# Seven products for every pair of row blocks in a mixture-of-experts stage, with each chunk's first sums on VectorE

## The chip, the cores and the metric

The kernel runs on one core of one Trainium2 chip. The core has a matrix engine (TensorE), a vector engine (VectorE, DVE in the profile), a scalar engine (ScalarE, ACT), a general engine (GpSimd, POOL) and a queue engine for transfers (SyncE, SP). Each engine works through its own queue in order, and semaphores tie the queues together. The metric is the time of one execution on the device, in microseconds; times of several executions are given by their median.

## The reference

The program is a sorted block attention followed by a dense mixture of eight experts. The attention gives 3072 rows `x` of 512 numbers. A softmax over the gate `x @ w_gate` is balanced by eight rounds of row and column normalisation, which gives weights `P`. All experts see all rows:

```python
out = np.zeros((N, D), dtype=np.float32)       # N, D, E, F = 3072, 512, 8, 1024
for e in range(E):
    h = np.maximum(x @ w1[e], 0.0)
    ye = h @ w2[e]
    out += P[:, e:e + 1] * ye
```

The first product is `x @ w1[e]` (512 deep, 1024 wide), the second `h @ w2[e]` (1024 deep, 512 wide). Everything the change touches lies in this loop, for experts 1 to 7; expert 0 is worked off beside the attention.

## The kernel before

The rows are cut into three chunks of 1024 (`p` = 0, 1, 2). For each expert and chunk the hidden tile `hT` is made in four units (`hidden`, i = 0 to 3) of seven products each, after the scheme of Strassen and Winograd: the matrices are seen as 2 x 2 blocks, and seven block products of sums take the place of eight. One product is two matmuls of 512 columns. The seven go into three PSUM banks of the pool `bk` (5 banks); ScalarE copies partial sums out (L502, L510, L515) and makes the last block (L524), VectorE makes the three other blocks by adding such a copy to a bank (L506 after product 2, L518 after product 5, L521 after product 6). The sums of weights that this needs are made by GpSimd (`sum_w`, L330), those of `x` by VectorE (`sum_x`, L434).

The second product of a chunk has four units too, i = 0 to 3. A unit makes two row blocks of 128 rows, `i` and `4 + i` (a pair), and comes in two forms:

- `output` (L536) is the plain form: two times eight matmuls of 512 columns (L542), each group in one bank of the pool `op` (3 banks). When a group is done, `gather` (L529) multiplies it by the expert's weight column and adds it to the output rows `osbl` on VectorE, 512 wide.
- `output7` (L561) uses seven products of four matmuls, 256 columns each (L573), on two banks: `u`, on which products 1, 3, 5 and 7 accumulate with a 256-wide gather after each, and `x`, whose left half takes product 2 and whose right half products 4 and 6; the right half is gathered after product 4, the whole bank (512 wide) after product 6. Product 3 needs the sum `s2` of four hidden blocks, 4 needs `s1`, 5 needs `s3`, 6 needs `s4`. `sum_h` (L553) makes the four on GpSimd, each 512 elements a partition (4 blocks f of 128), and `sum_w2` (L423) makes the sums of `w2`.

The sums s1 to s4 of unit i need all of `hT`, thus the last `hidden` unit of the chunk. The main loop (L639) takes the hidden units of chunk n and the second product's units of chunk n - 1 side by side: `take` alternates one step of each. At i = 0 the second product is plain, since the sums of that unit could only start when `hT` is complete; for i = 1 to 3 GpSimd makes the sums one unit ahead (`sum_h(i + 1, ...)`). In the first chunk (n = 1) and the last chunk all four units are plain. So of 84 units 57 use seven products and 27 are plain.

GpSimd's queue also holds the loads of `w1` and `w2` (L84, L89) for the expert after the next, at the start and the end of the chunk in which an expert begins, and the weight sums, which `sums` deals out at one a unit, three in the last unit. Matmuls, VectorE's work and the sums of `hT` may be moved by the scheduler within what their data allow; the loads and the weight sums are pinned to the order of the program.

Of the kernel before, what the change touches and what calls it, by code (L numbers as in the profile page):

```python
# [14 lines left out]
BF16 = mybir.dt.bfloat16  # L15
# [10 lines left out]
def kernel(  # L26
# [11 lines left out]
    nc = tc.nc  # L38
# [43 lines left out]
    def load_w1(e):  # L82
        w1t[e] = wp.tile([128, 4, F], BF16, name="w1e")
        pin(nc.gpsimd.dma_start(out=w1t[e],  # L84
                                in_=moe_w1[e].rearrange("(kk k) f -> k kk f", k=128)))

    def load_w2(e):
        w2t[e] = (wq if e else wcp).tile([128, 8, Dm], BF16, name="w2e")
        pin(nc.gpsimd.dma_start(out=w2t[e],  # L89
                                in_=moe_w2[e].rearrange("(fb k) f -> k fb f", k=128)))  # L90
# [231 lines left out]
    def sum_w(e):  # L322
        wct[e] = (wcq if e % 2 == 0 else wcp).tile([128, 3, 2, F // 2], BF16, name="wc")
        for kk in range(2):
            a11, a21 = (w1t[e][:, kk, f:f + 512] for f in (0, 512))
            a12, a22 = (w1t[e][:, 2 + kk, f:f + 512] for f in (0, 512))
            s1, s2, s4 = (wct[e][:, j, kk, :] for j in range(3))
            for a, b, o, c in ((a21, a22, ALU.add, s1), (s1, a11, ALU.subtract, s2),
                               (a11, a21, ALU.subtract, a21), (a12, s2, ALU.subtract, s4)):
                pin(nc.gpsimd.tensor_tensor(out=c, in0=a, in1=b, op=o))  # L330
                yield
# [83 lines left out]
    def sum_w2(e):  # L415
        w2s[e] = (wcp.tile([128, 4, 4, Dm // 2], BF16, name="w2e") if e % 2 else
                  w2q.tile([128, 4, 4, Dm // 2], BF16, name="w2s"))
        for k in (0, 2):
            b11, b12 = (w2t[e][:, k:k + 2, d:d + 256] for d in (0, 256))
            b21, b22 = (w2t[e][:, 4 + k:6 + k, d:d + 256] for d in (0, 256))  # L420
            t1, t2, t3, t4 = (w2s[e][:, j, k:k + 2, :] for j in range(4))
            for a, b, c in ((b12, b11, t1), (b22, t1, t2), (b22, b12, t3), (b21, t2, t4)):
                pin(nc.gpsimd.tensor_tensor(out=c, in0=a, in1=b, op=ALU.subtract))  # L423
                yield
# [111 lines left out]
    def output(e, p, i, hT):  # L536
        for j in range(2):
            tt = 4 * j + i
            t = 8 * p + tt
            oacc = op.tile([128, Dm], F32, name="oacc")  # L540
            for fb in range(8):
                nc.tensor.matmul(oacc, hT[:, fb, tt * 128:(tt + 1) * 128],  # L542
                                 w2t[e][:, fb, :], start=(fb == 0), stop=(fb == 7))
                if fb % 2 and fb < 7:
                    yield
            gather(e, t, 0, oacc)
            store(e, t)
            yield
# [1 line left out]

    hs = {}

    def sum_h(i, hT):  # L553
        s = hs[i] = hsp.tile([128, 4, 4, 128], BF16, name="hs")
        a11, a21, a12, a22 = (hT[:, f:f + 4, t + 128 * i:t + 128 * i + 128]
                              for f in (0, 4) for t in (0, 512))
        for a, b, o, c in ((a21, a22, ALU.add, 0), (s[:, 0], a11, ALU.subtract, 1),
                           (a11, a21, ALU.subtract, 2), (a12, s[:, 1], ALU.subtract, 3)):
            nc.gpsimd.tensor_tensor(out=s[:, c], in0=a, in1=b, op=o)  # L559

    def output7(e, p, i, hT):  # L561
        a, b = 8 * p + i, 8 * p + 4 + i
# [37 lines left out]
    def scale0(ts):  # L600
        for t in ts:
            nc.scalar.activation(out=osbl[:, t, :], in_=osbl[:, t, :], func=AF.Copy,
                                 scale=glog[:, t, 0:1])

    def take(works):
        while works:
            works = [w for w in works if next(w, 0) is None]
# [18 lines left out]
            next(xs, 0)  # L626
    take([chain, xs])
    xs = sum_x(2)
    last = (1, 0, hT)
    queue = [sum_w2(1)]  # L630

    def sums(n):
        while n and queue:
            if next(queue[0], 0) is None:
                n -= 1
            else:
                queue.pop(0)

    for n in range(1, 3 * (E - 1)):  # L639
        e, p = 1 + n // 3, n % 3  # L640
        if n == 1 or p == 0 and e + 1 < E:
            load_w1(e + 1)
            queue.append(sum_w(e + 1))
        hT = htp.tile([128, 8, 1024], BF16, name="hT")
        for i in range(4):
            if last[0] == 1:
                scale0([8 * last[1] + i, 8 * last[1] + 4 + i])
            if n > 1 and i < 3:
                sum_h(i + 1, last[2])
            next(xs, 0)  # L650
            sums(3 if n == 1 or i == 3 else 1)
            take([hidden(e, p, i, hT),
                  (output7 if n > 1 and i else output)(*last[0:2], i, last[2])])
        if n == 1 or p == 0 and e + 1 < E:
            load_w2(e + 1)
            queue.append(sum_w2(e + 1))
        last = (e, p, hT)
    for i in range(4):
        take([output(*last[0:2], i, last[2])])


# [28 lines left out]
```

## Time and profile before

| | us |
|---|---|
| median of 3 runs (lowest, highest) | 690.83 (690.35, 691.81) |
| the profiled execution | 690.48 |
| its span in the profile | 688.7 |
| TensorE matmul busy | 666.7 (97%) |
| VectorE busy | 474.5 (69%) |
| ScalarE busy | 298.0 (43%) |
| GpSimd busy | 432.4 (63%) |
| last plain units, L542 x64 | 13.98, from 670.08 |

A group's line in the profile gives source line, engine, operation, output and input tiles, shapes and count, then busy time with the mean of one in ns, then the idle time before the group and what ended it. A timeline's line gives start, duration, engine, line and operation. Matmuls are pipelined, so their single durations overlap; distances between starts say more. Idle time of an engine that is not the bottleneck costs nothing.

### The profile page before, as it was taken

Reading aid. Unit: us, or ns where it says so; the run is one execution under the profiler, and the core shown is the slowest. Engines: PE = TensorE matmul, PEld = TensorE weight load, DVE = VectorE, ACT = ScalarE, POOL = GpSimd, SP = SyncE. Lnnn points to the kernel's source line nnn. Section 1 sums busy time; section 2 is a strip of 40 time slices with the busy share of each in tenths; the row PEclk is TensorE's granted clock in tenths of the full one; section 3 lists DMA queues with packets and bytes.
Section 4 is the critical chain, followed back from the end, with each engine's and each line's share of the span. In section 5 each row is a group of like instructions: output and inputs, shape, how many; then the busy total and the mean of one; then the engine's idle time right before and its main releaser. Section 6 shows DMA issues by size and latency. Waiting matters only on the chain.

```text
span 688.7 us, 12265 instructions
## 1 busy us (share of the span) xinstructions
PE 666.7 (97%) x4784; PEld 404.4 (59%) x4784; DVE 474.5 (69%) x968; ACT 298.0 (43%) x550; POOL 432.4 (63%) x411
## 2 busy tenths in 40 slices
PE   2999999999999999999999999999999999999997
PEld 1757666644446556556656655655665665565563
DVE  6627555578757778667767776767776777676773
ACT  3747646345953333343333433333333433334330
POOL 4532324202737987978977987789795998637520
PEclk9899999999999999999999999999999999999999
DMA  9897833403210340030302140034003120001213
GB/s 146 164 218 120 140 77 63 62 1 62 30 32 1 62 61 1 1 63 9 54 0 35 28 62 1 1 62 61 1 1 62 25 38 0 1 1 63 91 65 151
DMA packets 31755, 36.51 MB, mean 53 GB/s; under 512 B 2000, under 2 KB 24016, under 8 KB 31696
## 3 DMA queue, kind: packets, MB, share of 16 engines
q0 software_dynamic: 26400, 27.82, 25.5%
q1 hardware_dynamic: 5296, 7.90, 3.4%
q8 instruction: 37, 0.61, 0.4%
q14 instruction: 22, 0.18, 0.1%
HBM read 52.45 MB, written 6.29 MB: 85 GB/s over the span
## 4 chain that ended last, share of the span: by engine, by line
PE 91%; DVE 5%; ACT 1%; DMA 1%; issue 1%; SPq 0%; DVEq 0%
PE bk L482 36%; PE oacc L573 25%; PE oacc L542 13%; PE bank L297 5%; PE bank L304 5%; PE bank L232 2%; PE bank L152 1%; PE bank L243 1%; PE bank L215 1%; PE bank L196 1%; DMA vsb<-vs 1%; DVE cs L464 0%; PE bk L297 0%; PE bk L466 0%; PE bank L183 0%
## 5 line engine op out<-in xcount | busy, mean ns | idle before, releaser
L529 DVE SCALAR_TENSOR_TENSOR osbl<-oacc,glog,osbl 128x256 f32<-128x256 f32 (+1 forms) x396 | 214.8, 554 | 122.4 <-PE oacc L542 61.3
L559 POOL TENSOR_TENSOR hs<-hT 128x512 bf16<-128x512 bf16 x114 | 130.0, 1154 | 63.0 <-DVE hT L521 62.8
L482 PE MATMUL bk<-xtT,w1e 128*128 128x512 bf16 x504 | 149.9, 379 | 0.2 <-ACT u L510 0.2
L573 PEld LDWEIGHTS <-hs 128*128 128x128 bf16 x912 | 89.2, 98 | 59.0
L542 PE MATMUL oacc<-w2e,hT 128*128 128x512 bf16 x432 | 119.8, 379 | 0.0
L524 ACT ACTIVATE hT<-bk 128x512 bf16<-128x512 f32 x84 | 50.1, 597 | 153.0 <-PE bk L482 152.9
L482 PE MATMUL bk<-xc,wc 128*128 128x512 bf16 x336 | 99.9, 379 | 0.0
L573 PEld LDWEIGHTS <-hT 128*128 128x128 bf16 x684 | 66.9, 98 | 44.2
L510 ACT COPY u<-bk 128x512 f32<-128x512 f32 x84 | 49.2, 586 | 92.9 <-PE bk L482 92.8
L573 PE MATMUL oacc<-w2e,hs 128*128 128x256 bf16 x588 | 88.2, 273 | 0.0
L573 PE MATMUL oacc<-w2e,hT 128*128 128x256 bf16 x576 | 86.4, 273 | 0.0
L482 PEld LDWEIGHTS <-w1e 128*128 128x128 bf16 x672 | 65.8, 98 | 30.5 <-issue 1.4
L542 PEld LDWEIGHTS <-hT 128*128 128x128 bf16 x432 | 42.3, 98 | 50.8
L506 DVE CUSTOM_DVE_ANT_0 hT<-bk,p 128x512 bf16<-128x512 f32 x84 | 58.0, 691 | 18.4 <-PE bk L482 14.8
L559 POOL TENSOR_TENSOR hs<-hT,hs 128x512 bf16<-128x512 bf16 x57 | 65.8, 1154 | 1.5
L559 POOL TENSOR_TENSOR hs<-hs,hT 128x512 bf16<-128x512 bf16 x57 | 65.7, 1152 | 0.0
L502 ACT COPY p<-bk 128x512 f32<-128x512 f32 x84 | 49.2, 586 | 31.3 <-PE bk L482 31.3
L482 PEld LDWEIGHTS <-wc 128*128 128x128 bf16 x504 | 49.3, 98 | 22.2
L518 DVE CUSTOM_DVE_ANT_0 hT<-bk,p 128x512 bf16<-128x512 f32 x84 | 57.8, 688 | 4.5 <-PE bk L482 1.4
L515 ACT COPY p<-bk 128x512 f32<-128x512 f32 x84 | 49.3, 586 | 25.4 <-PE bk L482 25.4
L521 DVE CUSTOM_DVE_ANT_0 hT<-bk,u 128x512 bf16<-128x512 f32 x84 | 57.3, 682 | 0.1
L482 PE MATMUL bk<-xc,w1e 128*128 128x512 bf16 x168 | 50.0, 379 | 0.0
(106 smaller groups left out, 777.6 us busy)
## 6 DMA issues: line engine op xcount, KB each, us to landing
w1e<-in_moe_w_dram POOLq DMA_DIRECT2D x8, 1024.0 KB, 8.2
w2e<-in_moe_w_dram POOLq DMA_DIRECT2D x8, 1024.0 KB, 8.9
out_dram<-osbl SPq DMA_DIRECT2D x24, 256.0 KB, 2.0
vt<-in_v_dram POOLq DMA_DIRECT2D x3, 768.0 KB, 10.6
vsb<-vs SPq DMA_DIRECT2D x16, 97.5 KB, 4.6
vsb<-vs POOLq DMA_DIRECT2D x16, 97.5 KB, 4.1
qt<-in_q_dram POOLq DMA_DIRECT2D x4, 384.0 KB, 12.8
kt<-in_k_dram POOLq DMA_DIRECT2D x4, 384.0 KB, 13.4
```

Of the source, the lines that this page charges most:

```text
L482: nc.tensor.matmul(ps, wa[:, kk, :], xa[:, kk, :], start=(first and kk == 0), stop=(kk == 1), skip_group_check=True)
L502: nc.scalar.copy(p1, u)
L506: nc.vector._custom_dve(TENSOR_ADD_SAT, out=c11, in0=w, in1=p1, s0=TOP, s1=0.0)
L510: nc.scalar.copy(u2, u)
L515: nc.scalar.copy(p5, v)
L518: nc.vector._custom_dve(TENSOR_ADD_SAT, out=c22, in0=u, in1=p5, s0=TOP, s1=0.0)
L521: nc.vector._custom_dve(TENSOR_ADD_SAT, out=c12, in0=v, in1=u2, s0=TOP, s1=0.0)
L524: nc.scalar.activation(out=c21, in_=u, func=AF.Relu)
L529: nc.vector.scalar_tensor_tensor(out=o, in0=ps, scalar=glog[:, t, e:e + 1], in1=o, op0=ALU.mult, op1=ALU.add)
L542: nc.tensor.matmul(oacc, hT[:, fb, tt * 128:(tt + 1) * 128], w2t[e][:, fb, :], start=(fb == 0), stop=(fb == 7))
L559: nc.gpsimd.tensor_tensor(out=s[:, c], in0=a, in1=b, op=o)
L573: nc.tensor.matmul(ps, h[:, fb, :], w[:, fb, :], start=(first and fb == 0), stop=(fb == 3), skip_group_check=True)
```

## The change

All 84 units of the second product use `output7`. The four plain units at the start and the end of the experts and the plain unit 0 of each chunk in between are gone.

The sums of unit 0 are made by VectorE, in two parts: those of blocks f = 0 to 2 (384 elements a partition, four operations), which need the first three hidden units only, are issued beside unit 3 of the chunk before, and those of f = 3 (128 elements, four operations) beside unit 0 itself. `sum_h` gets the range of f and the engine as arguments and becomes a generator that yields after each operation. Units 1 to 3 keep their sums on GpSimd.

The hidden units of all chunks become one stream, `ahead`, which is started two products before the second product's first unit; each step of `output7` is then followed by one product of that stream, and by one sum of `mine` where there is one. The last chunk has no hidden work beside it. The eight sums of `w2` of expert 1 are made before the loop. Loads keep their place by chunk.

```diff
-    def sum_h(i, hT):
-        s = hs[i] = hsp.tile([128, 4, 4, 128], BF16, name="hs")
-        a11, a21, a12, a22 = (hT[:, f:f + 4, t + 128 * i:t + 128 * i + 128]
+    def sum_h(i, hT, f0=0, f1=4, eng=nc.gpsimd):
+
+        if f0 == 0:
+            hs[i] = hsp.tile([128, 4, 4, 128], BF16, name="hs")
+        s = hs[i][:, :, f0:f1]
+        a11, a21, a12, a22 = (hT[:, f + f0:f + f1, t + 128 * i:t + 128 * i + 128]
                               for f in (0, 4) for t in (0, 512))
         for a, b, o, c in ((a21, a22, ALU.add, 0), (s[:, 0], a11, ALU.subtract, 1),
                            (a11, a21, ALU.subtract, 2), (a12, s[:, 1], ALU.subtract, 3)):
-            nc.gpsimd.tensor_tensor(out=s[:, c], in0=a, in1=b, op=o)
+            eng.tensor_tensor(out=s[:, c], in0=a, in1=b, op=o)
+            yield
...
-    last = (1, 0, hT)
     queue = [sum_w2(1)]
+
+    def run(*works):
+        for w in works:
+            for _ in w:
+                pass
...
-    for n in range(1, 3 * (E - 1)):
-        e, p = 1 + n // 3, n % 3
-        if n == 1 or p == 0 and e + 1 < E:
-            load_w1(e + 1)
-            queue.append(sum_w(e + 1))
-        hT = htp.tile([128, 8, 1024], BF16, name="hT")
+    sums(8)
+    run(sum_h(0, hT, 0, 3, nc.vector))
+    hTs = {0: hT}
+
+    def hiddens():
+        for n in range(1, 3 * (E - 1)):
+            hTs[n] = htp.tile([128, 8, 1024], BF16, name="hT")
+            yield from units(1 + n // 3, n % 3, hTs[n])
+
+    ahead = hiddens()
+    for _ in range(2):
+        next(ahead)
+    for n in range(1, 3 * (E - 1) + 1):
+        e, p, hT = 1 + (n - 1) // 3, (n - 1) % 3, hTs[n - 1]
+        d = 2 + n // 3
+        fetch = n == 1 or n % 3 == 0 and d < E
+        if fetch:
+            load_w1(d)
+            queue.append(sum_w(d))
+        if n == 3 * (E - 1):
+            run(sum_h(0, hT, 3, 4, nc.vector), sum_h(1, hT), sum_h(2, hT))
         for i in range(4):
-            if last[0] == 1:
-                scale0([8 * last[1] + i, 8 * last[1] + 4 + i])
-            if n > 1 and i < 3:
-                sum_h(i + 1, last[2])
+            if e == 1:
+                scale0([8 * p + i, 8 * p + 4 + i])
             next(xs, 0)
-            sums(3 if n == 1 or i == 3 else 1)
-            take([hidden(e, p, i, hT),
-                  (output7 if n > 1 and i else output)(*last[0:2], i, last[2])])
-        if n == 1 or p == 0 and e + 1 < E:
-            load_w2(e + 1)
-            queue.append(sum_w2(e + 1))
-        last = (e, p, hT)
-    for i in range(4):
-        take([output(*last[0:2], i, last[2])])
+            mine = iter(())
+            if n < 3 * (E - 1):
+                if i < 3:
+                    run(sum_h(i + 1, hT))
+                sums(3 if i == 3 else 1)
+                if i == 0:
+                    mine = sum_h(0, hT, 3, 4, nc.vector)
+                elif i == 3:
+                    mine = sum_h(0, hTs[n], 0, 3, nc.vector)
+            elif i == 1:
+                run(sum_h(3, hT))
+            for _ in output7(e, p, i, hT):
+                next(ahead, 0)
+                next(mine, 0)
+        if fetch:
+            load_w2(d)
+            queue.append(sum_w2(d))
```

## The prediction

> **What bounds the kernel now.** I read the windows by stage first, then the groups of instructions, then the timelines of single engines. Window lines give start:end, length, then busy time (and count) of matmul, weight load, VectorE, ScalarE and GpSimd, then clock, DMA share and GB/s.
>
> ```profile
> 249.00:274.00 25.00, 25.00 (x160) 15.50 (x159) 18.33 (x34) 9.42 (x16) 21.09 (x19) 1.00 0.28 43
> ```
> ```profile
> L559 POOL TENSOR_TENSOR hs<-hT 128x512 bf16<-128x512 bf16 x114 | 130.0, 1154 | 63.0 <-DVE hT L521 62.8
> L542 PE MATMUL oacc<-w2e,hT 128*128 128x512 bf16 x432 | 119.8, 379 | 0.0
> ```
>
> In the expert stage TensorE is busy 25.00 of 25.00 us at full clock, VectorE 18.33, GpSimd 21.09; matmuls wait for nothing. So only less TensorE work can shorten the stage, and anything that makes TensorE wait lengthens it. The 432 matmuls of L542 are 27 units of 16: the units still done plainly.
>
> What a plain unit costs against a seven-product one is read from the starts of the first product's first matmul, one unit apart:
>
> ```profile
> 645.37 0.59 PE L482 MATMUL bk<-xtT,w1e 128*128 128x512 bf16 x2
> ...
> 651.85 0.59 PE L482 MATMUL bk<-xtT,w1e 128*128 128x512 bf16 x2
> ...
> 657.93 0.59 PE L482 MATMUL bk<-xtT,w1e 128*128 128x512 bf16 x2
> ```
>
> The plain unit (with its first product) takes 6.48 us, the seven-product one 6.08: 0.40 us a unit, and steps of 6.08/7 = 0.87 us.
>
> Next, what happens when VectorE runs an operation with two SBUF inputs while GpSimd runs its sums:
>
> ```profile
> 163.38 0.68 DVE L434 TENSOR_TENSOR xc<-xtT,xc 128x1024 bf16<-128x1024 bf16 x1
> ...
> 175.27 1.60 DVE L434 TENSOR_TENSOR xc<-xtT 128x1024 bf16<-128x1024 bf16 x1
> 176.80 0.68 DVE L506 CUSTOM_DVE_ANT_0 hT<-bk,p 128x512 bf16<-128x512 f32 x1
> ...
> 181.72 1.30 DVE L434 TENSOR_TENSOR xc<-xtT,xc 128x1024 bf16<-128x1024 bf16 x1
> ```
> ```profile
> 171.51 1.36 POOL L423 TENSOR_TENSOR w2e<-w2e 128x512 bf16<-128x512 bf16 x1
> ...
> 175.18 1.16 POOL L423 TENSOR_TENSOR w2e<-w2e 128x512 bf16<-128x512 bf16 x1
> 176.29 1.61 POOL L423 TENSOR_TENSOR w2e<-w2e 128x512 bf16<-128x512 bf16 x1
> ...
> 181.32 1.15 POOL L330 TENSOR_TENSOR w1e<-w1e 128x512 bf16<-128x512 bf16 x1
> 182.44 1.60 POOL L330 TENSOR_TENSOR wc<-w1e,wc 128x512 bf16<-128x512 bf16 x1
> ...
> 645.26 2.27 POOL L559 TENSOR_TENSOR hs<-hT 128x512 bf16<-128x512 bf16 x2 [11.18 <-DVE hT L521]
> ```
>
> With GpSimd idle the operation takes 0.68 us. The one of 175.27 began 0.09 us into a GpSimd sum that ended at 176.34, and itself ended 0.53 us after that, at 176.87; the GpSimd sum behind it, issued at 176.29, took 1.61 instead of 1.15. The pair at 181.32/181.72 does the same. The two engines take turns, whole instructions at a time. Operations with an input in PSUM (the 0.68 of L506) aren't touched. The last line: at a chunk's end GpSimd sits idle until L521 of the chunk's last unit is done (644.51 + 0.68 = 645.19) and starts 0.07 us later.
>
> **The change part by part.** The sum is made against the profiled execution, 690.48 us (span 688.7 and 1.8 around it); the median shown is 690.83, 0.35 more, added at the end.
>
> *27 plain units become seven-product units.* 23 of them (4 of the first chunk, 19 first units) have first products beside them: 23 x 0.40 = 9.2 us less. The last 4 are costed with the tail.
>
> *VectorE's added work.* A unit gets five 256-wide gathers and one 512-wide instead of two 512-wide; issue to issue they take 0.40 (662.74 to 663.14) and 0.67 (178.03 to 178.70), so 2.67 for 1.34. The sums of unit 0 are four operations on f 0..2 (384 elements) and four on f 3 (128) a chunk. Neither shape is in the trace. L470, 192 fp32 elements with both inputs in SBUF, takes 0.27 issue to issue and L434 shows two bf16 elements a cycle against it (1024 in 0.60), so 0.27 for 384 is the nearest row, 0.39 (L463) the upper end; for 128, 0.13 with 0.26 (L124, 64 elements) as upper end. I take 0.27 and 0.13: 1.6 us a chunk. VectorE then has 3 x 0.60 + 2.67 = 4.5 us in units of 6.08: enough on average.
>
> *Where these sums stand.* In the built order the f-3 sums are not in unit 0 but in the last steps of the unit before: L521 (last unit), gather of product 5, s1, gather 6, s2, s3, gather 7, L506 of the new unit, gather 1, s4, gather 3. That is where GpSimd, released by the same L521, starts its sums. Count from the start of that last unit, with delays as in the trace (gather ready 0.64 after its product starts, L506/L518/L521 1.17 after the step starts). L521 runs from 3.91 and ends 4.60; gather 5 to 4.91; GpSimd's first sum 4.67 to 5.83, so s1 waits to 5.83, ends 5.95; gather 6 to 6.62; s2 waits for GpSimd's second sum to 7.07, ends 7.20; s3 waits for the third, 8.31, ends 8.44; gather 7 to 8.8; L506 to 9.4; gather 1 to 9.85. Product 3 accumulates on the bank that gather 1 reads and wants to start at 6.08 + 1.74 = 7.82. TensorE waits 2.06 us, with all queued products behind it. s4 waits again (to 10.8) but holds only gather 3, with room left. Without waits gather 1 would end at 7.4: a slack of some 0.4 us, no stall.
>
> The second of two sums in a row (s2, s3) is the disputed price: no row shows two. If VectorE keeps its turn s3 ends 7.33 and TensorE waits 1.06. I take 2.06, since in both rows the engine that was already waiting got in first.
>
> [...]
>
> Nineteen boundaries: 9 of this kind. At 5 the w1 load's issue (0.79) stands ahead of GpSimd's sums: s1 is free and ends 5.04, s2 at 6.5, s3 at 7.7, gather 1 at 9.2, a stall of 1.4. At 5 the w2 load's issue (0.93) stands third on GpSimd: s3 needn't wait and ends 7.33, a stall of 1.1. 9 x 2.06 + 5 x 1.4 + 5 x 1.1 = 31.0 (16.5 if pairs keep their turn).
>
> *The f 0..2 sums* stand one unit earlier, 17 us into the chunk (19 with the stall). GpSimd has 12 sums of hidden tiles and up to 6 of weights, 18 x 1.115 from -1.4, so it is done at 19 to 20: mostly idle by then. A single wait beyond the 0.4 slack costs up to 0.9; I take 2 us over 16 chunks (0 to 14).
>
> *First chunk.* Here VectorE's eight sums and one L434 meet GpSimd's eight sums L423 (from 169.16, back to back). Four f 0..2 sums and three f-3 sums ahead of product 3 at up to 1.1 each, with 2 to 3 us of slack: 5 us (2.8 to 7.5).
>
> *Tail.* Before: 64 plain matmuls in 13.98 us. After: no first product lies between, so each accumulation waits for its gather (0.2 + 0.48 + 0.06 after the product). From product 3 of a unit: product 5 ends 1.18 later, 6 at 1.61, whose 512-wide gather lets the next unit's product 2 start at 2.62, and products 2, 4 and 3 end at 3.9, against 3.45 for a plain unit. Ahead of the first product 3 lie s2, s3 and s4, alternating with GpSimd: it starts 10.2 after the last unit's start (8.0 if pairs keep their turn). The end then comes at 24.4 (22.1); the trace has 20.84 (664.01 to 684.85), less 0.87 for the two products that run earlier: 4.4 us later (2.2).
>
> *At nothing.* GpSimd's 24 more sums (27 us) lie in its idle time (62.8 us behind L521). The fourth sum tile a chunk reuses one freed a unit earlier. The w1 and w2 loads' issues keep their place by chunk; the w1 sums need their load 8.2 us later, and GpSimd gets to them in time in all but the first chunk, counted above. Stores on SP and L602 on ScalarE keep their order; ScalarE is busy 9.4 of 25. First product two ahead: the same matmuls, and their L518/L521 now follow gathers 3 and 4; no added wait by the delays above.
>
> Sum: 690.48 + 0.35 - 9.2 + 31.0 + 2 + 5 + 4.4 = 724.
>
> **The rivals.**
> *VectorE keeps its turn in pairs.* For it: 0.07 us overlap between VectorE's instructions. Against: GpSimd's overlap by 0.05 and lost the turn. 690.8 - 9.2 + 16.5 + 6.4 + 2.8 + 2.2 = 709.5 (6.4: 16 chunks x 0.4, since the sums of f 0..2 fall earlier against GpSimd).
> *The sums are hidden (faster).* If small operations don't wait, or slip in where GpSimd starts, and VectorE loses under 0.8 us between L521 and gather 1, TensorE stays full: 690.8 - 9.2 + 1.2 (tail) = 683. For it: L470 at 171.50 wasn't delayed, only the sum behind it (1.36). Against: there it came 0.01 us ahead of the sum; s1 comes 0.24 behind.
> *Both boundaries collide.* If the f 0..2 sums too meet a busy GpSimd in all 16 chunks, four waits less slack, some 1.5 us: 724 + 16 x 1.4 = 746. Against: GpSimd's count of 18.
>
> **How the numbers follow.** Forecast 0.52, pairs keep their turn 0.25, hidden 0.12, both boundaries 0.08, and 0.03 for gain and waits about equal. The forecast's own range is 715 to 735 from the bounds of its terms. The range from 703 to 735 takes in the second case with its bounds and leaves out 683 and 746. Changes under 0.2% can't be told from none. Slower 0.85, same 0.02, faster 0.13.
>
> **What would show it.** TensorE idle at product 3 of each chunk's first unit, released by VectorE's gather, 1 to 2 us, some 19 times, and none in the other units; VectorE's new sums of 128 elements at 0.5 to 1.3 us instead of 0.2; GpSimd sums at 1.25 or more where they now all take 1.15; a seven-product unit still 6.08 us elsewhere. The prediction is wrong if those sums stay short, or if the gather of product 1 isn't behind them.

## The result

| | us (lowest to highest) |
|---|---|
| kernel before, median of 4 runs | 691.20 (690.35 to 691.81) |
| changed kernel, median of 4 runs | 809.08 (806.80 to 811.37) |
| ratio, 95% interval | 1.1707 (1.1671 to 1.1742) |
| profiled execution of the changed kernel, its span | 808.92, 807.2 |

The change makes the kernel 17% slower. The prediction had the sign and the engine right and the size wrong: 724 us, with 703 to 735 as its range.

The page of the changed kernel: busy time of the matmuls, of VectorE and of GpSimd, the granted TensorE clock in 40 slices, and the head of the chain that ended last.

```profile
PE 681.9 (84%) x5031; PEld 444.8 (55%) x5108; DVE 656.4 (81%) x1244; ACT 298.4 (37%) x550; POOL 459.6 (57%) x435
...
PEclk9699999998997979979998989999899979999999
...
PE 51%; DVE 13%; issue 10%; POOL 1%; ACT 0%; DVEq 0%
PE oacc L577 27%; PE bk L482 24%; DVE hs L562 6%; DVE osbl L529 5%; DVE hT L506 2%; POOL hs L562 1%; DVE hT L518 0%; DVE hT L521 0%; DVE xtT L434 0%; ACT p L502 0%; DVEq L529 0%
```

TensorE is at 84% instead of 97%, VectorE's sums (L562) and its gathers behind them now stand in the chain, and the clock row has dips all through the expert stage.

The windows show it by chunk (columns as before: matmul, weight load, VectorE, ScalarE, GpSimd, clock, DMA share, GB/s). The first window is a chunk at whose start a `w1` load is issued, the second one without a load.

```profile
336.00:373.00 37.00, 26.41 (x164) 17.07 (x166) 31.29 (x44) 9.33 (x16) 20.65 (x20) 0.82 0.16 29
734.00:760.00 26.00, 24.25 (x166) 16.39 (x168) 23.18 (x45) 9.43 (x16) 13.38 (x13) 1.00 0.17 62
```

So there are two kinds of chunk. One without a load takes 26.06 us from boundary to boundary (first sums of the fourth block at 706.72 and 732.78); four units at 6.08 would be 24.32. One with a load takes 31 to 37 us, and part of it runs at half clock (0.82 on average in the first window).

The groups, with the shapes apart: GpSimd's sums, then VectorE's sums of the fourth block (128 elements) and of the first three (384).

```profile
L562 POOL TENSOR_TENSOR hs<-hT 128x512 bf16<-128x512 bf16 x126 | 144.1, 1159 | 173.9 <-DVE hT L521 142.0
L562 DVE TENSOR_TENSOR hs<-hT,hs 128x128 bf16<-128x128 bf16 x21 | 52.7, 2511 | 0.1
L562 DVE TENSOR_TENSOR hs<-hs,hT 128x128 bf16<-128x128 bf16 x21 | 47.6, 2266 | 0.0
L562 DVE TENSOR_TENSOR hs<-hT 128x128 bf16<-128x128 bf16 x42 | 35.6, 852 | 0.0
L562 DVE TENSOR_TENSOR hs<-hT 128x384 bf16<-128x384 bf16 x42 | 16.7, 397 | 0.0
```

Sums of a third of the length take two to six times as long on average (0.85 to 2.5 us against 0.40). Most of that isn't work but waits: the shortest take 0.21 us.

VectorE in a chunk without a load, with s1 to s4 of the fourth block, and the matmuls that wait behind them one chunk later:

```profile
706.72 1.01 DVE L562 TENSOR_TENSOR hs<-hT 128x128 bf16<-128x128 bf16 x1
...
708.31 0.52 DVE L562 TENSOR_TENSOR hs<-hs,hT 128x128 bf16<-128x128 bf16 x1
...
708.76 1.19 DVE L562 TENSOR_TENSOR hs<-hT 128x128 bf16<-128x128 bf16 x1
...
711.25 0.92 DVE L562 TENSOR_TENSOR hs<-hT,hs 128x128 bf16<-128x128 bf16 x1
```
```profile
737.45 0.60 PE L577 MATMUL oacc<-w2e,hs 128*128 128x256 bf16 x4 [1.59 <-DVE osbl L529]
```

This is the prediction's walk: s1 takes 1.0 us, s2 0.5, s3 1.2 (it loses its turn), s4 0.9, and TensorE then waits at product 3 for the gather.

A chunk with a `w1` load, GpSimd and then VectorE:

```profile
334.44 0.79 POOL L84 DMA_DIRECT2D w1e<-in_moe_w_dram  x1 [5.88 <-PE bk L482]
335.26 1.17 POOL L562 TENSOR_TENSOR hs<-hT 128x512 bf16<-128x512 bf16 x1
...
345.25 1.14 POOL L423 TENSOR_TENSOR w2e<-w2e 128x512 bf16<-128x512 bf16 x1
```
```profile
334.53 0.22 DVE L562 TENSOR_TENSOR hs<-hT 128x128 bf16<-128x128 bf16 x1
335.32 11.15 DVE L562 TENSOR_TENSOR hs<-hs,hT 128x128 bf16<-128x128 bf16 x1
346.39 0.21 DVE L562 TENSOR_TENSOR hs<-hT 128x128 bf16<-128x128 bf16 x1
```

s1 runs while GpSimd is in the issue and takes 0.22. s2 asks at 335.32, just after the first GpSimd sum has begun, and does not get in behind it, nor behind any of the nine that follow. It ends when GpSimd's run of ten is out, at 346.39 (345.25 + 1.14). TensorE stands for 10.43 us, until 348.05. In all ten chunks with a load, and in the first chunk, one sum waits like this: 11.15 us twice and 5.61 three times behind a `w1` load (5.61 where the run breaks off after five sums, since the next one waits for the load to land), 8.36 to 8.37 five times behind a `w2` load (a run of eight), 5.57 in the first chunk.

After so long a stall the matmuls come back slow. The first groups behind s4's wait for a `w2` load at 467.38, for comparison a group 3.8 us later:

```profile
476.19 1.01 PE L577 MATMUL oacc<-w2s,hs 128*128 128x256 bf16 x4 [6.79 <-DVE osbl L529]
477.00 1.06 PE L482 MATMUL bk<-xc,w1e 128*128 128x512 bf16 x2
...
480.01 0.59 PE L482 MATMUL bk<-xtT,w1e 128*128 128x512 bf16 x2
```

For 3.4 us a group takes 1.01 to 1.06 instead of 0.60, at a granted clock of 0.50 (from 472.8, 3.4 us into the stall, to 479.5; 1.00 before and after). Behind the stalls of 1.59, 2.23 and 2.63 us the clock stays at 1.00 (windows from 711.4, 215.2 and 177.38). In the ten other stalls of 4.89 to 10.44 us the 0.50 begins between 2.0 and 5.1 us after the start of the stall; what sets it off, no run shows.

### The profile page after: what moved, and what is told of

It is laid out like the page before. It is cut to its first block, busy times and chain, and to the rows that moved or that the text cites. A ratio compares the mean times of both kernels' runs of the same rounds, so it can differ in the third digit from the quotient of the medians.

```text
span 807.2 us, 13205 instructions
## 1 busy us (share of the span) xinstructions
PE 681.9 (84%) x5031; PEld 444.8 (55%) x5108; DVE 656.4 (81%) x1244; ACT 298.4 (37%) x550; POOL 459.6 (57%) x435
## 4 chain that ended last, share of the span: by engine, by line
PE 51%; DVE 13%; issue 10%; POOL 1%; ACT 0%; DVEq 0%
PE oacc L577 27%; PE bk L482 24%; DVE hs L562 6%; DVE osbl L529 5%; DVE hT L506 2%; POOL hs L562 1%; DVE hT L518 0%; DVE hT L521 0%; DVE xtT L434 0%; ACT p L502 0%; DVEq L529 0%
## 5 line engine op out<-in xcount | busy, mean ns | idle before, releaser
L529 DVE SCALAR_TENSOR_TENSOR osbl<-oacc,glog,osbl 128x256 f32<-128x256 f32 (+1 forms) x504 | 262.1, 523 | 69.9 <-PE oacc L577 65.2
L562 POOL TENSOR_TENSOR hs<-hT 128x512 bf16<-128x512 bf16 x126 | 144.1, 1159 | 173.9 <-DVE hT L521 142.0
L577 PEld LDWEIGHTS <-hs 128*128 128x128 bf16 x1344 | 135.8, 101 | 192.4 <-issue 105.6
L577 PE MATMUL oacc<-w2e,hs 128*128 128x256 bf16 x912 | 144.0, 284 | 52.6 <-DVE osbl L529 43.4
L577 PEld LDWEIGHTS <-hT 128*128 128x128 bf16 x1008 | 99.8, 99 | 67.6 <-issue 6.7
L577 PE MATMUL oacc<-w2e,hT 128*128 128x256 bf16 x864 | 130.9, 274 | 1.8 <-DVE osbl L529 1.1
L577 PE MATMUL oacc<-w2s,hs 128*128 128x256 bf16 x432 | 68.2, 283 | 44.3 <-DVE osbl L529 43.9
L562 POOL TENSOR_TENSOR hs<-hT,hs 128x512 bf16<-128x512 bf16 x63 | 72.6, 1152 | 1.6
L562 POOL TENSOR_TENSOR hs<-hs,hT 128x512 bf16<-128x512 bf16 x63 | 72.8, 1156 | 0.1
L518 DVE CUSTOM_DVE_ANT_0 hT<-bk,p 128x512 bf16<-128x512 f32 x84 | 58.0, 690 | 5.9 <-PE bk L482 2.5
L423 POOL TENSOR_TENSOR w2e<-w2e 128x512 bf16<-128x512 bf16 x32 | 37.0, 1172 | 44.1 <-PE oacc L304 43.7
L562 DVE TENSOR_TENSOR hs<-hT,hs 128x384 bf16<-128x384 bf16 (+1 forms) x42 | 61.2, 1456 | 0.1
L506 DVE CUSTOM_DVE_ANT_0 hT<-bk,p 128x512 bf16<-128x512 f32 x84 | 57.6, 686 | 4.2 <-PE bk L482 1.4
L502 ACT COPY p<-bk 128x512 f32<-128x512 f32 x84 | 49.3, 586 | 26.9 <-PE bk L482 26.9
L515 ACT COPY p<-bk 128x512 f32<-128x512 f32 x84 | 49.3, 587 | 25.5 <-PE bk L482 25.5
L521 DVE CUSTOM_DVE_ANT_0 hT<-bk,u 128x512 bf16<-128x512 f32 x84 | 57.2, 681 | 1.8 <-PE bk L482 1.8
L562 DVE TENSOR_TENSOR hs<-hs,hT 128x384 bf16<-128x384 bf16 (+1 forms) x42 | 55.3, 1318 | 0.0
```

What stands on the lines that cost most here:

```text
L502: nc.scalar.copy(p1, u)
L506: nc.vector._custom_dve(TENSOR_ADD_SAT, out=c11, in0=w, in1=p1, s0=TOP, s1=0.0)
L515: nc.scalar.copy(p5, v)
L518: nc.vector._custom_dve(TENSOR_ADD_SAT, out=c22, in0=u, in1=p5, s0=TOP, s1=0.0)
L521: nc.vector._custom_dve(TENSOR_ADD_SAT, out=c12, in0=v, in1=u2, s0=TOP, s1=0.0)
L529: nc.vector.scalar_tensor_tensor(out=o, in0=ps, scalar=glog[:, t, e:e + 1], in1=o, op0=ALU.mult, op1=ALU.add)
```

## Experiments

Theory A: all of the loss is VectorE's two-operand sums waiting for GpSimd's. Theory A1: the long waits need a load's issue ahead of GpSimd's sums. The rivals are in the expectations. Times are medians, each with its ratio to the kernel before on the same chip.

**One operand instead of two.**

```diff
+            if eng is nc.vector:
+                nc.vector.reduce_max(out=s[:, c].bitcast(F32),
+                                     in_=a.bitcast(F32).unsqueeze(3), axis=AX.X)
```

> The eight small VectorE operations of unit 0 in each chunk become maxima that read one SBUF operand in place of two, at the same shapes and places; so what stands for the sums of unit 0 is not the sums, that part of the computation is left out. Theory A (two-operand VectorE sums wait for GpSimd's sums): nothing of VectorE waits for GpSimd any more, operations of 128x128 take about 0.15 to 0.3 us, the stalls at product 3 of each unit 0 go, and the time is 680 to 688 us. Rival B (VectorE's in-order queue is what costs: the sums stand behind the evictions they wait for, whoever else is busy): the stalls stay, 800 to 812 us.

Measured: 688.24 us, 0.9965 (0.9953 to 0.9978), 0.24 us above A's range. The group of its 128x64 fp32 operations, which have the bytes of 128 bf16 values:

```profile
L563 DVE TENSOR_REDUCE hs<-hT 128x64 f32<-128x64 f32 x63 | 13.2, 211 | 0.0
```

A mean of 211 ns, no wait, and chunks of 24.31 us (s1 at 448.04 and at 618.23, seven chunks later): four units at 6.08, as counted. So A holds and B falls: in the chunks in the middle VectorE's queue and its additional time cost TensorE nothing; the sums with two SBUF operands do (26.06 us in a chunk of the changed kernel without a load). Only 2 of the 9.2 us arrive, since the first chunk (TensorE stalls of 2.62, 0.69 and 0.47 us, and 3.4 us in which groups take 1.06 instead of 0.59) and the tail (1.2 us longer) eat most of the rest. Operations of that size with one SBUF operand took 211 ns on average beside GpSimd's sums, those with two 852 to 2511 in the changed kernel. The run exchanged the operation along with its operands, a maximum for a sum; that it is the second operand alone is the author's reading.

**Loads issued later.** The first half of the change to the code:

```diff
-        if fetch:
+        if n == 1:
             load_w1(d)
...
+                if i == 1 and n > 1 and fetch:
+                    load_w1(d)
+                    queue.append(sum_w(d))
```

> The loads of the weights of experts 3 to 7 are issued behind GpSimd's sums of unit 2, where VectorE has no sums due, in place of ahead of the sums of unit 1; nothing else moves but the weight sums that wait for them. Theory A1 (a VectorE sum that meets the first GpSimd sum behind a load's issue waits until GpSimd's whole run of sums is out, any other waits for one instruction): the ten waits of 5.6 to 11.2 us go, all chunks come to about 26 us, and the time is 722 to 732 us. Rival A2 (the long waits come from the place in the chunk or from the transfers in flight, not from the issue ahead of the sums): waits over 5 us stay in these chunks or turn up where the transfers now run, and the time is 780 to 812 us.

Measured: 736.68 us, 1.0667 (1.0638 to 1.0696), 4.7 us above A1's range. The ten long waits are gone (that of the first chunk, whose load wasn't moved, stays: 5.57 us); VectorE at the boundary that took 11.15 us:

```profile
344.14 1.01 DVE L562 TENSOR_TENSOR hs<-hT 128x128 bf16<-128x128 bf16 x1
345.73 0.53 DVE L562 TENSOR_TENSOR hs<-hs,hT 128x128 bf16<-128x128 bf16 x1
346.19 1.18 DVE L562 TENSOR_TENSOR hs<-hT 128x128 bf16<-128x128 bf16 x1
348.68 0.91 DVE L562 TENSOR_TENSOR hs<-hT,hs 128x128 bf16<-128x128 bf16 x1
```

All boundaries in the middle now alternate. Chunks take 26.1 to 26.9 us rather than 26.06, since GpSimd's weight sums come later and some meet the sums of the first three blocks (0.46 to 1.30 instead of 0.35). A2 isn't dead yet: the transfers too were moved.

**Unit 0 plain, the new order kept.**

> The second product of unit 0 is in eight plain matmuls per half again in every chunk, and VectorE makes no sums; the order with the first product two products ahead stays, as do the seven products of units 1 to 3 in the first and last chunk. Theory A (all of the loss is the sums on VectorE): no chunk has a TensorE stall over 0.5 us, and the time is 688 to 696 us (before, less 3 x 0.4 in the first chunk, plus 2 to 4 us in the last). Rival C (the new order of the products costs by itself): over 700 us.

The edit drops both calls of `sum_h(0, ...)` on VectorE and takes `output` for i = 0. Measured: 694.98 us, 1.0062 (1.0041 to 1.0083). Chunks in the middle take 24.71 us (L542 at 403.58 and at 601.26, eight later), against the 24.72 before (6.48 + 3 x 6.08). So running two products ahead costs nothing in the middle, and C falls. The 4.7 us more lie in the first and last chunk.

**GpSimd behind VectorE.**

```diff
+        run(sum_h(0, hT, 3, 4, nc.vector))
+        gate = pin(nc.gpsimd.tensor_copy(held, hs[0][0:96, 3, 3, 0:2]))
+        with tc.issue_after(gate.ins):
+            run(sum_h(1, hT))
```

> GpSimd's sums of unit 1 wait until VectorE's last sum of unit 0 is made, so the two do not meet at the start of a chunk; all of the work is there. Theory A with A1: no VectorE sum of the fourth hidden block waits, the stalls at product 3 go, and the time is 684 to 698 us; GpSimd's sums come some 5 us later, and if they then meet VectorE's sums of the three other blocks in unit 3, each of these costs at most one GpSimd instruction (up to 1.2 us) and the time is up to 715 us. Rival D (the sums on VectorE are late in any case, GpSimd or not): over 725 us.

Measured: 706.49 us, 1.0237 (1.0219 to 1.0254), the upper part of A's range. All four sums of the fourth block take 0.21 (in the middle); but GpSimd, later now, meets three of the four sums of the first three blocks (0.64, 1.03 and 1.30), of which this is the last:

```profile
302.94 1.30 DVE L562 TENSOR_TENSOR hs<-hT,hs 128x384 bf16<-128x384 bf16 x1
```
```profile
304.70 0.60 PE L577 MATMUL oacc<-w2s,hs 128*128 128x256 bf16 x4 [0.90 <-DVE osbl L529]
```

The stall is 0.90 us here; most of the others are 0.68 or 0.69. Twelve of the chunks in the middle take 25.5 to 25.7 us, the other seven 24.2 to 24.3. D falls.

**What makes the long wait.** Two runs first, one that adds a cause and one that puts something between.

```diff
+        if not fetch and n > 1 and n % 3 != 1 or n in (19,):
+            pin(nc.gpsimd.dma_start(out=spare, in_=moe_w_gate.rearrange("(kk k) e -> k kk e", k=128)))
```

> A load of 4096 values into a spare tile is issued on GpSimd ahead of the sums of unit 1 in the chunks that had no load there, eight of them in the middle of the stage. Theory A1 (the issue ahead of a run of GpSimd sums is what makes a VectorE sum wait for the whole run): these chunks go from 26.06 us to between 31 and 37 us, as those with a w1 load had them, so 5 to 11 us more each, and the time is 845 to 900 us. Rival A2 (it is the large transfer in flight, or the waits for its landing): a load of this size changes nothing, 805 to 820 us.

Measured: 808.39 us, 1.1703 (1.1676 to 1.1729), no change from the changed kernel. By its expectation A1 had fallen, but the trace shows that the issue had nothing to wait for and ran at 394.19, 10 us ahead of the sums at 404.46. It had not tested what it was meant to.

```diff
             load_w1(d)
+            pin(nc.gpsimd.tensor_copy(held, Ibig[0:96, 0:2]))
```

> Behind each load of expert weights in the pair stage GpSimd makes a copy of 96x2 elements (under 0.2 us, one operand, waits for nothing) before its sums. Theory A1a (only the one instruction that follows an issue keeps VectorE out for the rest of the run, and the copy is done before a VectorE sum asks): the long waits go, as with the loads moved, and the time is 724 to 740 us. Theory A1b (after an issue the whole run keeps VectorE out, whatever comes first): the waits of 5.6 to 11.2 us stay, 800 to 815 us.

Measured: 810.57 us, 1.1734 (1.1717 to 1.1751): A1b. The copy stands at 335.79, right behind the issue, and a sum that asks at 335.88 still takes 11.25 us.

Then the additional load again, held back until the eviction that GpSimd's sums wait for:

```diff
+        if n > 4 and n % 3 == 2 or n in (18, 19):
+            pin(nc.gpsimd.tensor_copy(held, hT[0:96, 3, 512:514]))
+            pin(nc.gpsimd.dma_start(out=spare, in_=moe_w_gate.rearrange("(kk k) e -> k kk e", k=128)))
```

> A load of 4096 values into a spare tile is issued on GpSimd in eight chunks that had no load, and this time right ahead of the sums of unit 1: a copy of 96x2 elements in front of it waits for the same eviction as they do. In the earlier run with a small load the issue stood 10 us ahead of the sums, since it had nothing to wait for. Theory A1c (any issue right ahead of GpSimd's sums makes the VectorE sum that asks next wait for the whole run): these chunks go from 26.06 us to 31 to 37 us, and the time is 850 to 895 us. Rival A2 (only a large transfer does that): 807 to 820 us (the issue itself delays GpSimd by 0.8 us).

Measured: 890.88 us, 1.2901 (1.2876 to 1.2926), 82 us above the changed kernel: some 10 us in each of eight chunks. GpSimd and VectorE in one of them:

```profile
417.30 0.79 POOL L671 DMA_DIRECT2D spare<-in_moe_w_gate_dram  x1
...
418.12 1.17 POOL L562 TENSOR_TENSOR hs<-hT 128x512 bf16<-128x512 bf16 x1
```
```profile
417.31 0.21 DVE L562 TENSOR_TENSOR hs<-hT 128x128 bf16<-128x128 bf16 x1
418.11 11.21 DVE L562 TENSOR_TENSOR hs<-hs,hT 128x128 bf16<-128x128 bf16 x1
```

A load of 8 KB does it (11.21 us) as well as one of 1 MB (11.15): a large transfer isn't needed.

> The same with a load of 131072 values, a quarter of a weight load in as many rows. Theory A1c: as the small one, 850 to 895 us. Rival A2 (the transfer's size counts): waits of one to a few us at most, longer than with the small load, 815 to 850 us.

The same edit with `moe_w1[0][:, 0:256]`. Measured: 888.82 us, 1.2871 (1.2839 to 1.2903), and 11.21 us for the sum that waits: in these runs size doesn't matter, and A2, in which it does, falls.

> The quarter load again, issued one eviction earlier, some 2 us ahead of the sums of unit 1, so that its transfer runs while VectorE's sums ask, but GpSimd has finished the issue. Theory A1d (what counts is that VectorE asks within about 1 us of the issue's end): these chunks stay near 26 us, 807 to 815 us. Rival A2 (the transfer in flight is what counts): the waits appear as in the run with the quarter load right ahead, 815 us and over. If the next GpSimd sum behind any issue is what counts, however long after: 850 to 895 us.

The copy reads the first block's half of the unit's tile (L506) instead. Measured: 808.48 us, 1.1707 (1.1683 to 1.1731). The issue stood 3.3 us ahead of the sums:

```profile
402.34 0.79 POOL L671 DMA_DIRECT2D spare<-in_moe_w_dram  x1
405.63 1.14 POOL L562 TENSOR_TENSOR hs<-hT 128x512 bf16<-128x512 bf16 x1 [2.50 <-DVE hT L521]
```
```profile
405.85 1.01 DVE L562 TENSOR_TENSOR hs<-hT 128x128 bf16<-128x128 bf16 x1
```

With 2.50 us of idle time between issue and sums VectorE waits for one instruction only, with the transfer still under way or just done (3.8 us from issue to landing in the run before).

**How close, and what else.** The copy reads L518's half, one eviction ahead of the sums.

> The small load in eight chunks once more, now issued one eviction of VectorE (about 1 us) ahead of the point where the sums of unit 1 can start, so that a gap of a few tenths of a us lies between the issue's end and the first sum; with no gap these chunks took 35 us and more (890.9 us in all), with a gap of 2.5 us nothing changed (808.5 us). If the effect dies as soon as GpSimd stands idle for a moment: 806 to 815 us. If it lasts for at least a few tenths of a us: 850 to 895 us, and it is then the first sum of the fourth block that waits.

Measured: 808.89 us, 1.1704 (1.1674 to 1.1734), yet there was no gap at all:

```profile
406.28 0.79 POOL L671 DMA_DIRECT2D spare<-in_moe_w_gate_dram  x1
407.09 1.16 POOL L562 TENSOR_TENSOR hs<-hT 128x512 bf16<-128x512 bf16 x1
```
```profile
407.28 1.07 DVE L562 TENSOR_TENSOR hs<-hT 128x128 bf16<-128x128 bf16 x1
```

The first sum follows the issue by 0.02 us, s1 asks 0.19 us into it and waits for one instruction. So an issue right ahead of the sums isn't enough. In the eleven long waits of the changed kernel a two-operand VectorE operation had run inside the issue (s1, s3 or, in the first chunk, L434); here none had. The next run puts one there, a sum whose result nothing reads:

```diff
+                if i == 3 and k == 3 and (n > 3 and n % 3 == 1 and n < 18 or n in (17, 18)):
+                    pin(nc.vector.tensor_tensor(out=dum, in0=hTs[n][:, 0:3, 0:128],
+                                                in1=hTs[n][:, 0:3, 128:256], op=ALU.add))
```

> As the run with the small load issued about 1 us earlier, where the issue ended 0.02 us ahead of GpSimd's first sum and yet no VectorE sum waited for more than one instruction (808.9 us); in seven of its eight chunks VectorE now makes one more sum of 128x384, with a result that nothing reads, while GpSimd is in the issue. In all waits of 5.6 to 11.2 us so far a two-operand VectorE operation had run during the issue; in the runs with an issue but no such wait none had. Theory G (the issue ahead of the sums does it only together with a VectorE sum that runs during the issue): the first sum of the fourth block waits for the run in these seven chunks, about 10 us each, and the time is 860 to 890 us. Rival H (the VectorE sum in the issue is no cause; it is the sum's place behind the issue): 808 to 815 us.

The last clause on the earlier runs is wrong: in the run with the quarter load issued earlier two sums had run in the issue, and in the run with GpSimd behind VectorE sums had run in issues too; what both lacked was the direct succession. Measured: 810.50 us, 1.1730 (1.1696 to 1.1764). The added sum stood in the issue, but it held up L521, and GpSimd waited 0.26 us for that eviction between issue and sums. By the letter H; but it had changed two things at once.

The pair that followed removes the gap, with two more copies ahead of the issue, and adds a sum that asks early; the second kernel leaves the sum inside the issue out.

> In the last run the added VectorE sum pushed an eviction back, so that GpSimd stood idle for 0.26 us between the issue and its first sum. Now two more copies of 96x2 elements hold the issue back by 0.3 us, the added VectorE sum of 128x384 stands behind that eviction (inside the issue), and one more VectorE sum of 128x128 asks 0.3 us into GpSimd's first sum; nothing reads either. Theory G2 (a VectorE sum in the issue, and GpSimd going from the issue into its sums with no wait between): the second added sum waits for GpSimd's run, about 5 to 11 us, in seven chunks, and the time is 845 to 890 us. Rival H: it waits for one instruction, 810 to 820 us.

> The same without the VectorE sum inside the issue: GpSimd goes from the issue into its sums without a wait, and the added sum of 128x128 asks during the first of them. Theory G2: it waits for one instruction, 810 to 820 us. Rival H2 (no gap alone is enough): 845 to 890 us.

Measured: 886.68 us, 1.2825 (1.2773 to 1.2876), and 887.42 us, 1.2835 (1.2770 to 1.2901). Both have the long wait. But the added sum came earlier than meant: in the first kernel it asked 0.01 us before the issue's end. The second didn't serve as the control: without the first sum the other came 0.5 us into the issue, and was itself kept out from there on.

```profile
416.99 0.79 POOL L673 DMA_DIRECT2D spare<-in_moe_w_gate_dram  x1
417.80 1.16 POOL L562 TENSOR_TENSOR hs<-hT 128x512 bf16<-128x512 bf16 x1
```
```profile
417.50 11.49 DVE L694 TENSOR_TENSOR dum<-hT 128x128 bf16<-128x128 bf16 x1
```

The last run keeps the sum inside the issue and lets the next one ask well into GpSimd's first sum.

> As the run with the VectorE sum of 128x384 inside the issue and no gap, without the added sum of 128x128: the next VectorE sum to ask is the first of the fourth block, about 0.6 us into GpSimd's first sum. In the control of the last pair the added sum itself had begun inside the issue, so the pair did not tell. Theory G2 (a VectorE sum inside the issue sets GpSimd's whole run ahead of the next VectorE sum that meets it, whenever it asks in the first GpSimd sum): it waits for the run in seven chunks, 860 to 890 us. Rival W (what counts is that VectorE asks between the middle of the issue and some 0.2 us behind its end, with or without a sum before): it waits for one instruction, 808 to 820 us.

Measured: 887.57 us, 1.2848 (1.2810 to 1.2885): G2.

```profile
416.77 0.79 POOL L673 DMA_DIRECT2D spare<-in_moe_w_gate_dram  x1
417.58 1.17 POOL L562 TENSOR_TENSOR hs<-hT 128x512 bf16<-128x512 bf16 x1
```
```profile
416.89 0.35 DVE L695 TENSOR_TENSOR dum<-hT 128x384 bf16<-128x384 bf16 x1
...
418.21 10.57 DVE L562 TENSOR_TENSOR hs<-hT 128x128 bf16<-128x128 bf16 x1
```

It asks 0.63 us into the sum, later than s1 in the run without a sum in the issue, and waits 10.57 us. The two runs stand against each other with the same load and no gap: where a VectorE sum ran inside the issue and GpSimd went on into its sums without a wait, the next VectorE sum waits for the whole run. They differ in two copies and in when the sum asks as well, and a run in which nothing but the sum in the issue differs is missing. Other runs speak against these two as the reason: the run of 890.88 us has one copy, as that of 808.89, and the changed kernel's long waits began 0.06 and 0.63 us into a GpSimd sum, with the harmless 0.19 in between.

A sum inside the issue isn't the only way, though. In the first chunk of the run with one operand no two-operand VectorE operation ran in the issue (179.14 to 179.93). An L434, which has two operands there too, asked in the third sum behind it and still waited for the rest of the run (the last sum ended at 185.56, the L434 at 186.12); alone it takes 0.68:

```profile
182.19 1.15 POOL L566 TENSOR_TENSOR hs<-hs,hT 128x512 bf16<-128x512 bf16 x1
...
184.42 1.14 POOL L566 TENSOR_TENSOR hs<-hT,hs 128x512 bf16<-128x512 bf16 x1
```
```profile
182.45 3.67 DVE L434 TENSOR_TENSOR xc<-xtT,xc 128x1024 bf16<-128x1024 bf16 x1
```

The run with unit 0 plain has the same (2.99 us at 184.22). In both an L434 had met GpSimd's sums ahead of the issue, with no idle time of GpSimd from there to the wait; in the run of 808.89 GpSimd had been idle between VectorE's last sum and the issue. So what is shown is that the long wait comes with an issue in an unbroken stretch of GpSimd's work, and that such an issue alone doesn't make it; what else it takes is narrowed down, not settled.

**Towards a faster kernel.** If the sums never meet, 0.40 us a unit should be left. All four versions leave the first and last chunk plain and gate GpSimd as above; they differ in where VectorE's sums of the first three blocks stand and how many weight sums GpSimd makes behind them, behind a second gate.

> First and last chunk in plain matmuls; in the other 19 GpSimd's sums of unit 1 wait for VectorE's last sum (as in the gated run), and its weight sums at the end of a chunk wait for VectorE's sums of the first three blocks, which are traced two at a time behind products 2 and 3 of unit 3. Theory A: VectorE and GpSimd meet in hardly any sum, the chunks come to 24.3 to 24.7 us and the time is 680 to 687 us, under that of the kernel before. Rival E (four sums of 0.35 us in so short a stretch push the evictions behind TensorE's need, or GpSimd's later sums are late for units 1 to 3): 690 us and over.

> As the one before, but VectorE's sums of the first three blocks are traced one at a time behind products 1 to 4 of unit 3, and GpSimd's weight sums wait until the fourth. Theory A: 680 to 687 us; rival E, with the sums spread but GpSimd held up longer: late sums of units 1 to 3 or weight sums that meet VectorE's sums of the fourth block, 690 us and over.

Measured: 695.78 us, 1.0070 (1.0054 to 1.0085), and 695.13 us, 1.0064 (1.0051 to 1.0077): rival E in both. In the second:

```profile
350.25 0.94 DVE L562 TENSOR_TENSOR hs<-hT 128x128 bf16<-128x128 bf16 x1
```
```profile
354.01 0.60 PE L577 MATMUL oacc<-w2e,hs 128*128 128x256 bf16 x4 [0.68 <-DVE osbl L529]
```

The four weight sums reach into the fourth block's sums, and TensorE stalls 15 times in all, mostly for 0.68 us. (The two sums at a time had not come about: the order of VectorE's work was nearly the same in both.) Pinned in place, with three weight sums:

```diff
+            if i == 2 and n < N1 and n + 1 not in plain:
+                mine = sum_h(0, hTs[n], 0, 3, nc.vector, pin)
...
+                    for _ in range((0, 0, 0, 0, 1, 3, 0, 0)[k]):
+                        next(mine, 0)
```

> As the run with the sums two at a time, which lost 0.7 us in each of 15 chunks where VectorE's sums of the fourth block met weight sums: VectorE's four sums of the first three blocks now stand together, the last right behind the sixth gather of unit 2, and behind them GpSimd makes 3 weight sums (4 in every third chunk) instead of 4. Theory A: they are out before the fourth block's sums ask, most chunks have no TensorE stall over 0.3 us, and the time is 682 to 687 us. Rival E (the gathers behind the four sums come late for TensorE's third tile): a stall of 0.3 to 0.8 us moves there and the time is 688 to 697 us.

Measured: 688.83 us (12 runs), 0.9974 (0.9965 to 0.9983): faster than both kernels, if by little. In time that is E's range, without the stall that E had. A window of one chunk:

```profile
346.00:370.61 24.61, 24.61 (x170) 16.43 (x169) 20.69 (x45) 9.43 (x16) 19.33 (x20) 1.00 0.00 1
```

TensorE shows no stall, but the chunk takes 24.61 us, not 24.32. Two steps of 0.87 us are some 0.15 longer: TensorE begins product 3 at 375.27 where it was due at 375.14, just after the gather of product 1, which VectorE finished at 375.22 behind four sums.

> As the run before that beat the kernel before by 0.26%: its chunks took 24.61 us where four units of seven products take 24.32, since the gather that frees product 3's tile stands behind four VectorE sums, once for the first three blocks and once for the fourth. Now two of the four sums stand ahead of that gather and two behind it, both times. Theory A: the chunks come to 24.3 to 24.45 us and the time is 683 to 687 us. Rival F (GpSimd's runs end 0.5 us later in the chunk and meet VectorE's sums again): 688 us and over.

Measured: 691.40 us (12 runs), 1.0010 (0.9999 to 1.0020): rival F. GpSimd's run now ends later and the first sum of the three blocks meets it:

```profile
392.10 1.05 DVE L562 TENSOR_TENSOR hs<-hT 128x384 bf16<-128x384 bf16 x1
```

The best of these versions gets 1.6 us of the 7.6 that 19 units at 0.40 are worth.

## Why the prediction was wrong

*What bounds the kernel, and the gain: right.* With no wait a chunk takes 24.31 us in the run with one operand, so 0.40 us a unit.

*The price of a meeting: right.* Whole instructions, turn by turn (1.01, 0.52, 1.19 and 0.92 us for s1 to s4 from 706.72), with s3 losing its turn; the rival in which VectorE keeps it is out. The chunks without a load lose 1.74 us (26.06 less 24.32) where the walk had 2.06.

*The step that failed: the boundaries with a load,* "At 5 the w1 load's issue (0.79) stands ahead of GpSimd's sums: s1 is free ..., a stall of 1.4. At 5 the w2 load's issue ... a stall of 1.1." The sums that the walk set free did run free, and it then let the next one alternate as everywhere else. It waited for GpSimd's whole run. From s1 to s1 the five chunks with a `w1` load took 36.93, 37.47, 32.25, 30.65 and 31.04 us, 46.7 over 5 x 24.32, where 7.0 was counted; the five with a `w2` load 34.92, 33.50, 33.69, 34.54 and 34.80, 49.9 over, where 5.5 was counted. That is 84 of the 85 us between 724 and 809. Part of it is the half clock, a term that the sum, whose longest stall was 2.06 us, lacked altogether: the chunk from 463.81 lost 9.4 us with stalls of 0.61 and 6.79, so about 2 us.

*The other terms* nearly cancel: the chunks without a load came 2.4 us cheaper (8 x 1.74 and a stall of 2.23 in the second chunk, for 18.5), the sums of the first three blocks cost nothing behind the first chunk (0.35 each, GpSimd mostly idle as counted, against 2), and the first chunk was dearer (stalls of 2.63 and 5.27 us and a clock of 0.83 for 20 us, about 11 us, where 5 us in all was counted). The tail is 3.8 us longer, where 4.4 was counted: 23.85 us from the last hidden unit's first matmul (778.71) to the end of the last matmul, 20.05 before. VectorE's sums without a wait took 0.26 us to the next instruction for 384 elements (from 703.21) and 0.13 for 128 (from 334.53), as estimated from two rows (0.27 and 0.13); how many elements a cycle that is, no run shows.

*"Both boundaries collide"* (746) didn't happen, *"the sums are hidden"* (683) needs the one operand. Of what would show it, the stalls and the sums at 0.5 to 1.2 us were there; GpSimd's sums at 1.25 or more were not there at the boundaries (1.14 to 1.17): in these meetings VectorE alone pays.

*Could it have been read from the trace before?* Not the long wait: the only operations with two SBUF operands inside a load's issue there (32x64 fp32, from 2.55 to 7.54 us, 0.21 to 0.26 each) have no GpSimd sums behind the issue. But the prediction set the range around a price it had from meetings without an issue, and for ten of 19 boundaries an issue was the difference; the upper end should have held a run of GpSimd's sums, 5 to 11 us, there.

## What to carry to other kernels

Before giving VectorE operations with two SBUF operands beside GpSimd work, look up on the timeline what GpSimd does at that very time: here a meeting cost up to one GpSimd instruction (sums of 0.21 us took 0.52 to 1.19), and behind a load's issue on GpSimd it could cost its whole run (5.6 to 11.2 us). Make GpSimd wait for the VectorE sums (a copy of two elements a partition did, and they took 0.21), or keep the load's issue a few us away from them (0.53 to 1.18 with the loads later); with either the long waits were gone in the middle chunks. Stalls of 4.89 us and more were dearer here than their length, since TensorE ran at a granted clock of 0.50 behind them; those of 1.59 us were not (1.00).

## What the runs showed of the hardware that was not expected

- A two-operand VectorE sum that meets back-to-back GpSimd sums normally gets in behind the first (0.5 to 1.2 us for 0.21). After a DMA issue on GpSimd in which another VectorE sum ran, with GpSimd's sums straight behind, it waits until GpSimd's queue breaks off: 5.6 us with a run of five sums, 8.4 with eight, 11.2 with ten. Twice it did so with no VectorE sum in the issue (3.67 and 2.99 us for 0.68). The size of the transfer (8, 256, 1024 KB) made no difference (11.21, 11.21, 11.15 us), a copy in between didn't help (11.25), an idle gap of 0.26 or 2.5 us did (810.50 and 808.48 us in all, against 887.57 and 888.82 without), as far as one run each can tell. A sum that asked 0.5 us into an issue with GpSimd's sums straight behind was held as well (11.49), while those that asked in its first 0.3 us ran free (0.21 to 0.22, and 0.35 for 384 elements); in the run with GpSimd behind VectorE, where idle time follows the issue, sums that asked 0.71 and 0.84 us into it ran free too (0.21 to 0.22). So what follows the issue seems to count, not the issue by itself.
- Why it is so is open. In ordinary meetings a VectorE sum got in behind the one GpSimd instruction that was running (1.01 us for s1); here the wait spanned ten (11.15 us), and no run shows what holds the sum back.
